# The last row tile of an expert's first group is summed and split six steps behind the second tile instead of eight

## The chip, the cores and the metric

The kernel runs on one core of a Trainium2 chip. The metric is the device time of one execution in microseconds (us); lower is better. The time before is 987.38 us, the median of three executions (985.54 to 989.09).

## The reference, cut to what matters

The kernel computes an attention layer with 32 memory slots per head, and then a mixture of eight experts over its 4608 output rows `x` of 512 numbers, of which each row uses two:

```python
for e in range(E):                       # E = 8
    for k in range(2):
        mask = top2[:, k] == e
        h = np.maximum(x[mask] @ w1[e], 0.0)          # 512 -> 1024
        out[mask] += top2_w[mask, k, None] * (h @ w2[e])   # 1024 -> 512
```

Only the expert part is touched by the change.

## The kernel before, in words

The rows of each expert are collected in a list of at most 1216 slots. In the experts 1 to 7 that list is worked off in two groups, written (e, g) here: group 0 has 640 rows, group 1 has 576. Each group goes through these stages.

**Gathering and splitting the rows** (`gather_sums`, line 908). A group is taken as two halves that are multiplied together, so it has 320 (group 0) or 288 (group 1) columns, in three row tiles: two of 128, and a last one of 64 (group 0) or 32 (group 1). For each row tile POOL gathers two blocks, `gsum` and `gtile` (L920). VectorE (DVE) forms sums for a seven-product scheme (L937, L938, L952, L953). Then the tile is split in three parts, each into a high and a low fp16 half: `ghalf` from `gsum` (the rows as they are), `ghalf` from `gtile` (after L938), and `gsplit` from `gsum` (after L952 and L953). ScalarE (ACT) makes the high half (L947), DVE the low half (L948), and the DMA queue of SP transposes both into the buffer `xt` (L949).

**First product** (`mm1_sums`, line 964). TensorE (PE) forms seven products for each of four column blocks, six matmuls for each, of 288 or 320 columns (L978). Product 1 and 2 read the part of `xt` that comes from `ghalf<-gsum`, products 7 and 4 read that from `ghalf<-gtile`, and products 6, 5 and 3 read that from `gsplit`. Product 1 opens a PSUM tile named `ps`, product 2 one named `pb`, product 7 one named `mp`; product 6 adds to product 1's `ps`. The tuple `ORDER` (line 83) starts with products 1, 1, 2, 6, 2, 6, 7, 7. ACT reads the sums out (`r`, `s`, `yv`: L984, L1026), DVE combines them (`yw`, `yv`: L988), and the result becomes a high half `hh` (ACT, L991) and a low half `hl` (DVE, L992).

**Second product** (`mm2`, line 1072). PE multiplies `hh` and `hl` by the second weights (L1092), ACT scales the row tile into `y` (L1104), and POOL adds it to the output rows (L1122).

**Weights.** The weights of the next expert are loaded by SP (L742, 512 KB each) and prepared by ACT (L782 takes squares, L792 the high half) and DVE (L785, L795 the low half); one small product on PE (L406) lies in that chain.

**What sets the order.** The main loop emits the first product of one group and the second product of the same group in steps; `step_side` counts them in `ticks[0]` and after each one lets one of the side generators (gathering for later groups, weight preparation) emit a piece. `gather_sums` holds a row tile back until `ticks[0]` has reached `moved`, which is set to the current tick plus `MOVE` (8) when the tile before it has been emitted. `pace` makes a piece's first instruction wait for a matmul that was emitted some three steps earlier. A scheduler then orders the instructions of each engine by priority and by its own estimate of time, so what stands in a row on an engine is not the order of emission; each engine then runs its row in that order.

```python
            n, a, b, t = fetched[i]
            yield from until(max(t, moved))
```

Of the kernel before, what the change touches and what calls it, by code (L numbers as in the profile page):

```python
# [80 lines left out]
LAG, STEP, WAIT, FAR, MOVE, MORE = 2, 100, 8, 8, 8, ()  # L81
# [10 lines left out]
def tile_attn_moe(ctx, tc, q_t, phi_t, kv, wgn, noise, w1, w2, out):  # L92
# [809 lines left out]
    def pace(d):  # L902
        if len(paced) > LAG:
            tc.add_manual_dep(d.ins, paced[-1 - LAG].ins.name, SYNC, reason="pace")
# [3 lines left out]
    def gather_sums(e, g, free):  # L908
        nh, t0 = HALF[g], 5 * g
        fetched = {}  # L910

        def fetch(i):
            if i > 2:
                return
            n = 128 if i < 2 else nh - 256
            a = late["gs"].tile([128, 768], F32, name="gsum", bufs=2)
            b = mpool.tile([128, DM], F32, name="gtile", bufs=GT)
            for x, ix in ((a[:, 256:768], LT[e][:n, t0 + i if i < 2 else t0 + 4, 0:1]),
                          (b, LT[e][:n, t0 + 2 + i, 0:1] if i < 2 else LX[e][:n, g, 0:1])):
                G.indirect_dma_start(out=x[:n], out_offset=None, in_=xs[:, :],  # L920
                                     in_offset=bass.IndirectOffsetOnAxis(ap=ix.bitcast(I32), axis=0))
            fetched[i] = (n, a, b, ticks[0] + FAR)

        fetch(0)
        yield
        while not free():
            yield "wait"
        xt = XT[e, g] = late["xt"].tile([128, NX, nh], F16, name="xt%d" % g)
        moved = 0
        for i in range(3):  # L930
            fetch(i + 1)
            yield
            n, a, b, t = fetched[i]
            yield from until(max(t, moved))
            s1, a11, a12 = (a[:n, k:k + 256] for k in (0, 256, 512))
            a21, a22 = b[:n, 0:256], b[:n, 256:512]
            pace(V.tensor_tensor(s1, a21, a22, OP.add))  # L937
            V.tensor_tensor(a21, a11, a21, OP.subtract)  # L938
            yield
            for x, k, w in ((a[:n, 256:768], 0, 2), (b[:n], 2, 2), (a[:n], 4, 3)):  # L940
                if k == 4:
                    gh = late["gs"].tile([128, 2, 768], F16, name="gsplit", bufs=2)[:n]
                else:
                    halves[0] += 1
                    gh = late["gs"] if halves[0] % 3 == 0 else mpool
                    gh = gh.tile([128, 2, DM], F16, name="ghalf", bufs=1 if halves[0] % 3 == 0 else 2)[:n]
                pace(A.activation(gh[:, 0], x, AF.Copy))  # L947
                V.tensor_tensor(gh[:, 1], x, gh[:, 0], OP.subtract)  # L948
                nc.sync.dma_start_transpose(xt[:, 4 * k:4 * k + 4 * w, i * 128:i * 128 + n], gh.rearrange("p a d -> p (a d)"))  # L949
                yield  # L950
                if k == 0:
                    V.tensor_tensor(a11, s1, a11, OP.subtract)  # L952
                    V.tensor_tensor(a12, a12, a11, OP.subtract)  # L953
                    yield
            moved = ticks[0] + MOVE

    banks = [0]

# [178 lines left out]
    side, paced, ticks = [], [], [0]  # L1137

    def until(t):
        while ticks[0] < t:  # L1140
            yield "wait"
# [160 lines left out]
    def rows_in(k, e, g):  # L1302
        return gather_sums(e, g, lambda: k < opened[0]) if e else gather(e, g)
# [96 lines left out]
```

## Time and profile before

| | |
|---|---|
| median of three executions | 987.38 us (985.54 to 989.09) |
| the profiled execution | 984.07 us, of which the span from first to last instruction is 982.1 us |
| busy share of the span | PE 93%, DVE 64%, ACT 59%, POOL 35% |
| granted TensorE clock, mean | 0.98 of full speed |

The attention part takes about the first 290 us; from there to about 955 us PE works through the fourteen groups of the experts 1 to 7 almost without a gap, and a short end follows in which POOL writes the last rows.

### The profile page before, as it was taken

The numbers are of one execution on the slowest core, as the hardware profiler recorded it, in microseconds if no ns is written. First come the engines' busy times: TensorE is split into PE (matmuls) and PEld (weight loads), VectorE is DVE, ScalarE is ACT, GpSimd is POOL, SyncE is SP. The second block draws the span as 40 slices with busy tenths as digits, with TensorE's granted clock in tenths as the row PEclk, the third lists the DMA queues.
The fourth block names the chain that finished last, engine by engine and source line by source line (L and its number), as shares of the span: only waits on it lengthen the run. The fifth ranks groups of instructions, "written<-read, shape, count | busy, mean of one in ns | idle before, by whom it ended". The sixth has DMA issues, their size and how long they took to land.

```text
span 982.1 us, 17769 instructions
## 1 busy us (share of the span) xinstructions
PE 917.5 (93%) x6510; PEld 544.4 (55%) x6510; DVE 626.4 (64%) x1471; ACT 579.8 (59%) x1188; POOL 342.5 (35%) x310
## 2 busy tenths in 40 slices
PE   3898985999899999999999999999999999999994
PEld 2465653677446564646564646464656465656552
DVE  1557788655677585849574957595759575957240
ACT  2586775433547575758665765576567665765240
POOL 3121654724243324535453232323242324240302
PEclk9999987999999999999999999999999999999998
DMA  8999989874878576947795689577947784775403
GB/s 317 323 333 313 362 272 328 239 101 101 153 180 162 110 147 128 212 75 158 132 201 101 140 122 201 91 149 132 208 72 170 137 180 77 169 110 82 63 1 49
DMA packets 197720, 162.03 MB, mean 165 GB/s; under 512 B 151872, under 2 KB 162304, under 8 KB 195584
## 3 DMA queue, kind: packets, MB, share of 16 engines
q1 hardware_dynamic: 177952, 120.43, 50.1%
q0 software_dynamic: 19680, 40.45, 23.5%
q8 instruction: 52, 0.85, 0.4%
q14 instruction: 36, 0.29, 0.1%
HBM read 86.77 MB, written 41.07 MB: 130 GB/s over the span
## 4 chain that ended last, share of the span: by engine, by line
PE 63%; DVE 5%; DMA 5%; issue 3%; ACT 2%; POOL 1%; SPq 0%; POOLq 0%; ACTq 0%
PE ps L1092 19%; PE mp L1092 15%; PE ps L978 14%; PE mp L978 7%; PE pb L978 4%; DMA xt<-ghalf 3%; PE mp L1062 3%; DVE wl L795 1%; DMA gtile<-xs,ltall 1%; DVE wlx L795 1%; POOL out L1122 1%; DVE yw L988 1%; DVE yv L988 1%; DVE gsplit L948 0%; ACT wl L782 0%
## 5 line engine op out<-in xcount | busy, mean ns | idle before, releaser
L1122 POOL DMA_INDIRECT out<-y,ltall x80 | 135.3, 1691 | 258.8 <-ACT y L1104 228.9
L1092 PEld LDWEIGHTS <-hh 128*128 128x128 f16 (+2 forms) x1504 | 122.7, 99 | 144.4 <-issue 17.5
L978 PE MATMUL ps<-xt,wh 128*128 128x320 f16 (+1 forms) x560 | 139.2, 293 | 1.1 <-ACT s L984 0.7
L1092 PE MATMUL ps<-wl,hh 128*128 128x512 f16 (+2 forms) x400 | 125.8, 380 | 0.0
L1092 PE MATMUL ps<-wh,hl 128*128 128x512 f16 (+2 forms) x400 | 125.5, 380 | 0.0
L1092 PE MATMUL ps<-wh,hh 128*128 128x512 f16 (+2 forms) x400 | 122.7, 381 | 0.0
L1092 PE MATMUL mp<-wh,hh 128*128 128x512 f16 (+2 forms) x352 | 113.4, 380 | 0.5 <-DVE hh L1069 0.5
L1092 PE MATMUL mp<-wl,hh 128*128 128x512 f16 (+2 forms) x352 | 113.0, 380 | 0.0
L1092 PE MATMUL mp<-wh,hl 128*128 128x512 f16 (+2 forms) x352 | 112.3, 380 | 0.0
L978 PEld LDWEIGHTS <-wh 128*128 128x128 f16 x896 | 86.6, 98 | 41.5 <-issue 5.8
L1092 PEld LDWEIGHTS <-hl 128*128 128x128 f16 (+2 forms) x752 | 63.2, 99 | 68.9 <-issue 4.9
L978 PE MATMUL ps<-xt,whx 128*128 128x320 f16 (+1 forms) x336 | 96.4, 292 | 0.0
L792 ACT ACTIVATE wh<-stg,wsc 128x512 f16<-128x512 f32 x112 | 76.4, 713 | 31.7 <-DVE wsc L415 20.0
L920 POOL DMA_INDIRECT gtile<-xs,ltall x28 | 34.5, 1233 | 138.8 <-DVE ghalf L948 133.5
L978 PEld LDWEIGHTS <-whx 128*128 128x128 f16 x672 | 65.7, 98 | 27.2 <-issue 2.7
L795 DVE SCALAR_TENSOR_TENSOR wl<-stg,wsc,wh 128x1024 f16<-128x1024 f32 (+1 forms) x63 | 73.1, 1160 | 10.6 <-ACT wh L792 10.2
L978 PE MATMUL ps<-xt,wl 128*128 128x320 f16 (+1 forms) x280 | 72.8, 292 | 0.0
L782 ACT ACTIVATE wl<-stg 128x1024 bf16<-128x1024 f32 x56 | 58.6, 1047 | 23.9 <-DMA stg<-in_w 18.7
L978 PE MATMUL mp<-xt,wh 128*128 128x320 f16 (+1 forms) x224 | 64.9, 293 | 4.1 <-DMA xt<-ghalf 4.1
L709 POOL DMA_INDIRECT lst<-gent,gidx x54 | 54.5, 1009 | 36.2 <-DVE gidx L692 18.5
L920 POOL DMA_INDIRECT gsum<-xs,ltall x42 | 46.3, 1103 | 55.4 <-DVE gsplit L948 44.8
L978 PE MATMUL mp<-xt,whx 128*128 128x320 f16 (+1 forms) x224 | 64.9, 292 | 0.0
(245 smaller groups left out, 1886.8 us busy)
## 6 DMA issues: line engine op xcount, KB each, us to landing
stg<-in_w SPq DMA_DIRECT2D x64, 512.0 KB
kvs<-in_kv SPq DMA_DIRECT2D x16, 1024.0 KB
out<-zt SPq DMA_DIRECT2D x38, 256.0 KB
qs<-in_q_t SPq DMA_DIRECT2D x16, 576.0 KB
xs<-xr SPq DMA_DIRECT2D x36, 256.0 KB
phs<-in_phi_t SPq DMA_DIRECT2D x16, 288.0 KB
kvs<-in_kv SPq DMA_DIRECT2D x16, 128.0 KB
xt<-ghalf SPq DMA_TRANSPOSE x88
```

The source lines that it names most:

```text
L709: sc = G.indirect_dma_start(out=lst[:, :], out_offset=bass.IndirectOffsetOnAxis(ap=idx[:, j, k:k + 1], axis=0), in_=ent[:, j, k, :], in_of ...
L782: (id if first else pace)(A.activation(wl[:, c * 1024:c * 1024 + 1024].bitcast(BF16), s[c], AF.Square, accum_out=am[:, c:c + 1]))
L792: (id if first else pace)(A.activation(h[:, o + k:o + k + 512], x[:, k:k + 512], AF.Identity, scale=sc))
L795: V.scalar_tensor_tensor(l[:, o:o + n], x, sc, h[:, o:o + n], op0=OP.mult, op1=OP.subtract)
L920: G.indirect_dma_start(out=x[:n], out_offset=None, in_=xs[:, :], in_offset=bass.IndirectOffsetOnAxis(ap=ix.bitcast(I32), axis=0))
L978: mark["pe"] = T.matmul(ps[:, :nh], t[w][:, o:o + 128], xt[:, 4 * k0 + 2 * n0 * lo + 2 * (a - k0) + c, :nh], start=(first and m == 0), sto ...
L988: V.scalar_tensor_tensor(y[:, h, :nh], ps[:, :nh], SHC, x[:, :nh], op0=OP.mult, op1=OP.add)
L1062: d = mark["pe"] = mark["mm1", g] = T.matmul(ps[:, :n], ww[:, c * FF + f * 128:c * FF + (f + 1) * 128], xt[:, xo + c, :n], start=(k == 0), ...
L1092: mark["pe"] = T.matmul(ps[lo:lo + x.shape[-1]], x, ws, start=start, stop=stop)
L1122: d = G.indirect_dma_start(out=out[:, :], out_offset=bass.IndirectOffsetOnAxis(ap=LT[e][:n, t, 0:1].bitcast(I32), axis=0), in_=y[:n], in_o ...
```

## The change

`moved` is the tick at which the next row tile may be summed and split. The changed line sets it when a tile has been emitted; `i` is that tile's number. With `i` equal to 1 the next one is the last tile of the group. The value for `i` equal to 2 is never used, since the next group starts with `moved = 0`. So one tile in each of six groups, (2,0) to (7,0), may be emitted two ticks earlier.

```diff
@@ gather_sums
-            moved = ticks[0] + MOVE
+            moved = ticks[0] + (6 if i and e > 1 and g == 0 else MOVE)
```

Since the scheduler sees other priorities and other matmuls to wait for, rows move on all engines from that point of the program on, also later tiles and weight preparation. Three places show it.

On ACT, ahead of group (3,0), stand the readouts of (2,1)'s first product (`yv`, `hh`), the squares of expert 3's second weights (L782), the scaled rows of (2,1) (L1104), and the splits (L947) of (3,0)'s last tile, which are those of 64 rows. Before:

```order
L1026 ACTIVATE yv<-ps_5781 128x288
L782 ACTIVATE wl_5939,wam<-stg_5930 128x1024
L991 ACTIVATE hh<-yw 128x2x288
L991 ACTIVATE hh<-yv 128x2x288
L991 ACTIVATE hh<-yw 128x2x288
L782 ACTIVATE wl_5939,wam<-stg_5934 128x1024
L1104 ACTIVATE y<-ps_5922,wlu 128x512
L782 ACTIVATE wl_5939,wam<-stg_5932 128x1024
L947 ACTIVATE gsplit<-gsum 64x768
L782 ACTIVATE wl_5939,wam<-stg_5936 128x1024
L1104 ACTIVATE y<-ps_6003,wlu 128x512
L947 ACTIVATE ghalf<-gtile 64x512
```

And in the changed kernel, at the same place:

```order
L991 ACTIVATE hh<-yv 128x2x288
L947 ACTIVATE ghalf<-gtile 64x512
L991 ACTIVATE hh<-yw 128x2x288
L1026 ACTIVATE yv<-ps_5783 128x288
L947 ACTIVATE ghalf<-gsum 64x512
L782 ACTIVATE wl_5943,wam<-stg_5934 128x1024
L991 ACTIVATE hh<-yv 128x2x288
L991 ACTIVATE hh<-yw 128x2x288
L782 ACTIVATE wl_5943,wam<-stg_5938 128x1024
L947 ACTIVATE gsplit<-gsum 64x768
L782 ACTIVATE wl_5943,wam<-stg_5940 128x1024
L1104 ACTIVATE y<-ps_5926,wlu 128x512
```

The split of `gtile` has moved from behind the second L1104 to the middle of the `hh` rows, that of `gsplit` from behind the first L1104 and the third L782 to behind the second L782. The `ghalf<-gsum` split of this tile stood seven rows above the first row shown of before, and now stands between the `hh` rows too.

On DVE, at the same place, stand the combined products and low halves of (2,1) (L988, L992) and the sums and low halves of (3,0)'s last tile (64 rows). Before:

```order
L992 SCALAR_TENSOR_TENSOR hl<-yv,hh 128x2x288
L988 SCALAR_TENSOR_TENSOR yw<-mp,s_5850 128x288
L992 SCALAR_TENSOR_TENSOR hl<-yw,hh 128x2x288
L992 SCALAR_TENSOR_TENSOR hl<-yv,hh 128x2x288
L992 SCALAR_TENSOR_TENSOR hl<-yw,hh 128x2x288
L937 TENSOR_TENSOR gsum<-gtile 64x256
L938 TENSOR_TENSOR gtile<-gsum,gtile 64x256
L952 TENSOR_TENSOR gsum<-gsum 64x256
L953 TENSOR_TENSOR gsum<-gsum 64x256
L948 TENSOR_TENSOR gsplit<-gsum,gsplit 64x768
L785 TENSOR_REDUCE wam_6067<-wam 128x1
L948 TENSOR_TENSOR ghalf<-gtile,ghalf 64x512
```

And in the changed kernel:

```order
L937 TENSOR_TENSOR gsum<-gtile 64x256
L938 TENSOR_TENSOR gtile<-gsum,gtile 64x256
L988 SCALAR_TENSOR_TENSOR yw<-mp,s_5832 128x288
L992 SCALAR_TENSOR_TENSOR hl<-yv,hh 128x2x288
L948 TENSOR_TENSOR ghalf<-gtile,ghalf 64x512
L988 SCALAR_TENSOR_TENSOR yw<-mp,s_5852 128x288
L992 SCALAR_TENSOR_TENSOR hl<-yw,hh 128x2x288
L948 TENSOR_TENSOR ghalf<-gsum,ghalf 64x512
L952 TENSOR_TENSOR gsum<-gsum 64x256
L953 TENSOR_TENSOR gsum<-gsum 64x256
L992 SCALAR_TENSOR_TENSOR hl<-yv,hh 128x2x288
L992 SCALAR_TENSOR_TENSOR hl<-yw,hh 128x2x288
```

Six of the last tile's rows now stand ahead of the last two `hl` rows; its `gsplit` follows directly behind the rows shown.

On ACT, ahead of group (2,0), the first group that the change touches, the changed kernel has these rows (the names are as above, one expert earlier):

```order
L991 ACTIVATE hh<-yv 128x2x288
L947 ACTIVATE ghalf<-gtile 64x512
L991 ACTIVATE hh<-yw 128x2x288
L782 ACTIVATE wl_4879,wam<-stg_4874 128x1024
L947 ACTIVATE ghalf<-gsum 64x512
L782 ACTIVATE wl_4879,wam<-stg_4876 128x1024
L1104 ACTIVATE y<-mp,wlu 128x512
L782 ACTIVATE wl_4879,wam<-stg_4872 128x1024
L1104 ACTIVATE y<-ps_4944,wlu 128x512
L947 ACTIVATE gsplit<-gsum 64x768
L1104 ACTIVATE y<-mp,wlu 128x512
```

Here `gsplit` has changed places with `ghalf<-gtile`: it stands behind the second L1104, where `ghalf<-gtile` stood before.

## Rows read from the trace of the kernel before

**Rows 1.** Page, part 1: busy time, share of the span, instructions.

```profile
PE 917.5 (93%) x6510; PEld 544.4 (55%) x6510; DVE 626.4 (64%) x1471; ACT 579.8 (59%) x1188; POOL 342.5 (35%) x310
```

**Rows 2.** Waits of PE, 290 to 955 us: total, times, longest.

```profile
PE mp L978 <- DMA xt<-ghalf: 4.1, 3, 1.8
PE ps L978 <- ACT s L984: 0.7, 3, 0.3
```

**Rows 3.** Timeline of PE: start, duration, instruction, idle before it.

```profile
397.28 0.30 PE L978 MATMUL mp<-xt,wh 128*128 128x320 f16 x1
...
489.33 0.45 PE L978 MATMUL ps<-xt,wh 128*128 128x320 f16 x2
...
492.68 0.31 PE L978 MATMUL mp<-xt,wh 128*128 128x320 f16 x1 [0.73 <-DMA xt<-ghalf]
...
590.75 0.31 PE L978 MATMUL mp<-xt,wh 128*128 128x320 f16 x1 [1.83 <-DMA xt<-ghalf]
...
782.25 0.31 PE L978 MATMUL mp<-xt,wh 128*128 128x320 f16 x1 [1.55 <-DMA xt<-ghalf]
```

**Rows 4.** Timeline of SP's queue ahead of (3,0): start and duration of issue.

```profile
471.62 0.53 SPq L742 DMA_DIRECT2D stg<-in_w  x1
483.79 1.23 SPq L949 DMA_TRANSPOSE xt<-gsplit  x1
485.66 1.30 SPq L949 DMA_TRANSPOSE xt<-ghalf  x1
```

**Rows 5.** Chain that ended last: start, duration, what.

```profile
485.66 6.97 DMA xt<-ghalf
...
582.20 8.50 DMA xt<-ghalf
...
774.75 7.46 DMA xt<-ghalf
```

**Rows 6.** Timeline of DVE ahead of (3,0).

```profile
470.93 0.45 DVE L988 SCALAR_TENSOR_TENSOR yw<-mp,s 128x288 f32<-128x288 f32 x1
...
474.85 0.75 DVE L992 SCALAR_TENSOR_TENSOR hl<-yw,hh 128x576 f16<-128x576 f32 x1
478.38 0.42 DVE L937 TENSOR_TENSOR gsum<-gtile 64x256 f32<-64x256 f32 x1 [2.78 <-PE ps L1092]
...
482.81 0.95 DVE L948 TENSOR_TENSOR gsplit<-gsum,gsplit 64x768 f16<-64x768 f32 x1 [2.66 <-ACT gsplit L947]
...
484.94 0.69 DVE L948 TENSOR_TENSOR ghalf<-gtile,ghalf 64x512 f16<-64x512 f32 x1 [0.94 <-ACT ghalf L947]
```

**Rows 7.** Timeline of ACT ahead of (3,0).

```profile
477.61 1.06 ACT L782 ACTIVATE wl<-stg 128x1024 bf16<-128x1024 f32 x1 [2.99 <-DMA stg<-in_w]
...
480.32 0.69 ACT L1104 ACTIVATE y<-ps,wlu 128x512 f32<-128x512 f32 x1 [1.57 <-PE ps L1092]
...
481.95 0.83 ACT L947 ACTIVATE gsplit<-gsum 64x768 f16<-64x768 f32 x1
...
484.29 0.62 ACT L947 ACTIVATE ghalf<-gtile 64x512 f16<-64x512 f32 x1
```

**Rows 8.** Timeline of ACT ahead of (4,0).

```profile
576.87 0.69 ACT L1104 ACTIVATE y<-ps,wlu 128x512 f32<-128x512 f32 x1 [1.63 <-PE ps L1092]
...
580.84 0.62 ACT L947 ACTIVATE ghalf<-gtile 64x512 f16<-64x512 f32 x1
```

**Rows 9.** Timeline ahead of and in (2,0): ACT, DVE, SP, PE.

```profile
389.37 0.62 ACT L947 ACTIVATE ghalf<-gtile 64x512 f16<-64x512 f32 x1
...
390.02 0.68 DVE L948 TENSOR_TENSOR ghalf<-gtile,ghalf 64x512 f16<-64x512 f32 x1 [0.94 <-ACT ghalf L947]
...
390.73 1.27 SPq L949 DMA_TRANSPOSE xt<-ghalf  x1
...
400.27 0.30 PE L978 MATMUL ps<-xt,wh 128*128 128x320 f16 x1
```

**Rows 10.** Chain that ended last, a gather of 128 rows.

```profile
201.10 4.50 DMA gtile<-xs,ltall
```

## The prediction

> **What bounds the kernel now.** I read the page first: PE is busy for 93% of the span, the next engine for 64% [rows 1]. A change on ACT, DVE or the DMA queues can then give time back only where PE waits, so the second view is PE's own waits. From 290 us to 955 us, in which all fourteen groups are worked off, there are two kinds: three waits for the transpose `xt<-ghalf`, 4.1 us together, and three of at most 0.3 us for a readout of ACT, 0.7 us together [rows 2]. That is the whole stock from which this change can pay: 4.8 us, of which 4.1 us are of the kind that it touches.
>
> The timeline of PE says where they lie [rows 3]. All three stand before the first matmul into `mp`, which is product 7, the first reader of what comes from `ghalf<-gtile`: 0.73 us in group (3,0), 1.83 us in (4,0), 1.55 us in (6,0). Product 1 and 2 ran ahead of it without a wait. The same matmul of (2,0) at 397.28 us shows no wait.
>
> **What the late transpose is late for.** I followed (3,0) backwards. The transpose that PE waits for is issued at 485.66 us [rows 4] and takes 6.97 us to land; the other two take 8.50 and 7.46 us [rows 5]. It is issued late because its split is: DVE makes the low half at 484.94 us, ACT the high half at 484.29 us [rows 6, 7]. ACT does so only then because its row has three L782, two L1104 and `gsplit` ahead of it (the order shown with the change). The first L1104 waits 1.57 us for PE's second product of the group before, and the second L782 2.99 us for its weights [rows 7]. DVE, meanwhile, stood idle for 2.78 us before L937 of this tile, until a matmul that `pace` had named [rows 6]. So of the last tile's three parts `ghalf<-gtile` comes last, although it is read before `gsplit`. (4,0) shows the same picture: `ghalf<-gtile` at 580.84 us, 3.97 us behind the start of the first L1104 at 576.87 us [rows 8].
>
> **What the change does there.** It adds and removes no work. The same seven DVE and three ACT instructions and three transposes of the tile stand elsewhere, and two things follow.
>
> *The order of need is restored.* In five of the six groups `gtile` is now split ahead of `gsplit`. In the sixth, (4,0), the two stand one behind the other, both ahead of the third L782 and of every L1104. In (3,0) and (6,0), too, all three splits stand ahead of the first L1104. The split that PE waited for was made at 484.29 us, the first L1104 began at 480.32 us [rows 7], so it comes at least 3.97 us earlier in (3,0), and the same 3.97 us in (4,0) [rows 8]; the waits to cover are 0.73 and 1.83 us [rows 3].
>
> *A closer reckoning for (3,0).* In DVE's new row L937 and L938 (0.42 us each) stand ahead of the `yw` that began at 470.93 us [rows 6]. With that `yw` (0.45) and one `hl` (0.75) the low half of `gtile` begins near 470.93 + 0.84 + 0.45 + 0.75 = 472.97 us and ends 0.69 us later, at 473.7 us, where before it ended at 485.6 us. Its transpose, even at 8.50 us, lands by 482.2 us, over 9 us before its reader. `gsplit` stands on ACT behind the second L782, which began at 477.61 us when its weights had landed: 477.61 + 1.06 + 0.2 (its accumulator read, about) + 0.83 on ACT, then 0.95 on DVE [rows 6, 7] is 480.7 us. At 8.50 us it lands at 489.2 us. In PE's new row product 6 of (3,0), the first reader of `gsplit`, stands behind 37 matmuls, product 7 behind 18. Without its wait product 7 began at 492.68 - 0.73 = 491.95 us [rows 3]; 19 matmuls at 0.136 us ((400.27 - 397.28) / 22, from (2,0) [rows 3, 9], where 22 lie between) put product 6 at 494.5 us. That leaves 5.3 us.
>
> *The tightest group is (2,0).* There `gsplit` takes the place behind the second L1104 that `ghalf<-gtile` had (389.37 us). It is longer by 0.83 - 0.62 on ACT and by 0.95 - 0.68 on DVE [rows 6, 7, 9], so it is issued near 390.73 + 0.21 + 0.27 = 391.2 us and lands, with 6.97 to 8.50 us, between 398.2 and 399.7 us. Its reader stands behind 42 matmuls, two more than before: 400.27 + 0.27 = 400.5 us [rows 9]. Cover: 0.8 to 2.3 us. I count no wait there.
>
> So the three waits go: -0.73 - 1.83 - 1.55 = -4.11 us.
>
> **What it may cost.** Six of the tile's DVE rows now stand ahead of the last two `hl` of the second product's input: 4 x 0.42 + 2 x 0.69 = 3.06 us; on ACT two `ghalf`, 2 x 0.62 us, stand among the `hh`. Whoever needs `hl` is PE's L1092. The cover is the idle time of DVE behind the last `hl` (474.85 us), 2.78 us [rows 6], and the fact that PE shows no wait for `hl` at all [rows 2]; how far it is from one no row shows. The bounds are nothing and, with no cover, 3.06 us in each of six groups, 18.4 us. I take the value from the nearest row: PE's existing short waits are of 0.3 us at most [rows 2], and I allow two such, 0.5 us, for rows that moved. SP and POOL issue the same transfers; the last tile's transposes now stand ahead of nothing that PE waits for, since the loads of the next weights follow them as before.
>
> Sum: the profiled execution took 984.07 us, span 982.1 us and 2.0 us around it. 984.07 - 4.11 + 0.5 = 980.5 us. The runs shown have a median of 987.38 us, 3.31 us above that execution; carried over, 987.38 - 3.6 = **983.8 us**, 0.36% less.
>
> **The rivals.**
>
> 1. *The landing doesn't follow the issue.* Two transposes of (3,0) are issued 1.87 us apart [rows 4], and all three late ones take 7 to 8.5 us [rows 5], whatever their place: other transfers are in flight. If the landing is set by these, an earlier issue only lengthens the flight, the waits stay, and the time is 987.4 us. For it speaks the spread of the flights; against it, that the earliest bound, the landing of the weights issued at 471.62 us, is past by 477.61 us, when L782 could begin [rows 4, 7], 14 us before the reader. The Trainium skill (DMA: Bandwidth & Descriptors, section Queues, rings and completion order) says that a transfer's semaphore step lands only after every earlier write of that DMA engine, across its queues. By that rule, the earlier transposes would still not be held past the weights' landing; that the flights are long while much is in flight agrees with it.
>
> 2. *The gain is given back further on.* The whole row of ACT behind (2,0) is reordered. In (5,0), (6,0) and (7,0) a first 128-row split of the following group now stands among the last tile's rows. ACT would be held by a gather that has just been issued. A gather took 4.50 us in the chain [rows 10]; less the 2.99 us by which ACT already stood idle at such a place [rows 7], that is 1.5 us each, 4.5 us in all: 984.07 - 3.6 + 4.5 = 985.0 us, that is 988.3 us on the runs' scale.
>
> 3. *The sums delay the second product* (slower). Place: the last two `hl` on DVE, ahead of L1092. Price: 3.06 us less the part that is covered, in six groups. It decides from 4.11 / 6 = 0.7 us uncovered per group on: at 1.3 us each (a cover of 1.8 us) it is 984.07 - 4.11 + 7.8 = 987.8 us, 991.1 us on the runs' scale. For it: DVE and ACT run in the order of their rows, and the second L782 of ACT held everything behind it for 2.99 us [rows 7]. Against it: the idle 2.78 us of DVE directly behind [rows 6], and no PE wait on DVE in the list [rows 2]. The Trainium skill (TensorE: Matmul & The Clock Gate, section Architectural detail: the array is 16x 32x32, not 1x 128x128) calls the queues of ScalarE and VectorE strictly first in, first out. By that rule whatever stands ahead of `hl` delays it; the trace agrees for ACT.
>
> **How the numbers follow.** I give the forecast 0.62, rival 1 0.12, rival 2 0.13, rival 3 0.13. About 0.3% (3 us) is what a measurement of this kernel can tell from no change. Of the forecast's 0.62 I leave 0.04 below that bound, since 3.6 us is close to it. Faster: 0.58. Same: 0.04 + 0.12 + 0.13 = 0.29. Slower: 0.13. The forecast's own range is 979.3 to 985.3 us: below, all 4.8 us of waits go and with them the 3.3 us that the runs lie above the profiled execution; above, half of the 4.11 us stays. With rivals 1 and 2, at 987.4 and 988.3 us, the range is 979.3 to 989.1 us, the slowest run of before; it leaves out rival 3 and a little of the forecast.
>
> **What would show it.** In the changed kernel's profile: PE's list of waits from 290 us on has no `xt<-ghalf` wait of over 0.3 us, and none for `gsplit` in (2,0). The last tile's `ghalf<-gtile` ends on DVE near 473 to 474 us before (3,0), and its transpose is no piece of the chain any more. (3,0) begins as early as before, (4,0) by 0.7 us and (5,0) by 2.6 us earlier. If the list shows waits for `hl` or `hh` in L1092, rival 3 holds; if for `s`, `r` or `yv` behind a split in (5,0) to (7,0), rival 2; if the transposes are issued early and still land at the old time, rival 1. What would make it wrong: a change of the row order of PE itself that costs it time that no wait of before hints at, or a part of the 3.31 us between the profiled execution and the runs that comes from these very waits, in which case the gain is larger.

## The result and the profile after

The changed kernel takes 975.5 us, the median of four executions (974.04 to 979.31), beside 986.46 us (984.37 to 989.09, four executions) of the kernel before in the same series: a ratio of 0.9893, with a 95% interval of 0.9854 to 0.9933. In a later series it was 976.43 us (11 executions) beside 983.55 us (22), a ratio of 0.9946 (0.9924 to 0.9969). So it is faster, by 0.5 to 1.1%. (The ratios with their intervals are estimates from the executions of a series, not quotients of the two medians beside them; in the later series the quotient would be 0.9928.) One slow execution of a kernel below, `c2_before_free`, is left out of its median and range: 984.54 us, 1.6% above its fastest. The forecast, 983.8 us, had the direction right and the size too small; 975.5 us lies below its range.

The page of the changed kernel, part 1, answers to [rows 1]:

```profile
PE 912.0 (93%) x6510; PEld 545.2 (56%) x6510; DVE 626.2 (64%) x1471; ACT 580.9 (59%) x1188; POOL 346.8 (35%) x310
```

The same 6510 matmuls keep PE busy for 5.5 us less. PE's waits from 290 to 955 us (total, times, longest) answer to [rows 2]:

```profile
PE mp L1092 <- DVE yw L988: 1.9, 1, 1.9
PE ps L978 <- ACT s L984: 1.6, 4, 0.7
PE ps L1092 <- DVE hl L992: 0.3, 1, 0.3
PE ps L1092 <- ACT hh L991: 0.2, 1, 0.2
```

All three waits for `xt<-ghalf` are gone, as forecast. But other waits have come, 4.0 us in all against 4.8 us before: by this list the change should have paid 0.8 us.

To see what it paid I cut out of each execution the stretch from the first matmul of (1,0) to that of (7,1), which leaves aside what comes before the change and the end. A row of this view has the stretch, its length, and then busy time and count of PE, PEld, DVE, ACT and POOL. Of the kernel before:

```profile
299.02:923.91 624.89, 619.71 (x4070) 360.19 (x4070) 423.74 (x776) 397.35 (x730) 215.67 (x157) 1.00 0.73 137
```

And of the changed kernel:

```profile
300.68:919.22 618.54, 614.36 (x4071) 361.31 (x4070) 423.03 (x776) 398.80 (x730) 220.25 (x157) 1.00 0.76 139
```

The stretch is 6.35 us shorter. Only 1.0 us of that is idle time of PE (624.89 - 619.71 = 5.18 us, now 4.18 us); 5.35 us are busy time, for the same matmuls at the same granted clock (1.00, third from the end of the row).

**Where busy time can shrink.** The second product of a group has a last row tile of 64 or 32 rows per half. Its 48 matmuls are narrow (64 or 32 columns of weights). From the start of (4,1) to that of (5,0) PE has no wait in either kernel, yet this took 683.80 - 637.63 = 46.17 us before and 680.19 - 635.26 = 44.93 us after. PE's timeline of the kernel before there (start, duration, instruction; neighbours alike are drawn together, xN; `128*32` means 32 columns of weights, `128*128` the full width):

```profile
637.10 0.38 PE L1092 MATMUL ps<-wh,hl 128*64 128x512 f16 x2
637.31 0.38 PE L1092 MATMUL ps<-wl,hh 128*64 128x512 f16 x2
637.63 0.42 PE L978 MATMUL ps<-xt,wh 128*128 128x288 f16 x2
...
666.51 0.40 PE L1092 MATMUL ps<-wh,hh 128*32 128x512 f16 x4
666.73 0.39 PE L1092 MATMUL ps<-wh,hl 128*32 128x512 f16 x4
666.95 0.38 PE L1092 MATMUL ps<-wl,hh 128*32 128x512 f16 x2
667.26 0.39 PE L1092 MATMUL mp<-wh,hh 128*128 128x512 f16 x1
...
671.47 0.39 PE L1092 MATMUL ps<-wh,hh 128*32 128x512 f16 x1
671.79 0.39 PE L1092 MATMUL mp<-wh,hl 128*128 128x512 f16 x1
...
683.80 0.45 PE L978 MATMUL ps<-xt,wh 128*128 128x320 f16 x2
```

And of the changed kernel, where all 48 stand together:

```profile
635.26 0.42 PE L978 MATMUL ps<-xt,wh 128*128 128x288 f16 x2
...
676.95 0.38 PE L1092 MATMUL mp<-wh,hl 128*128 128x512 f16 x1
677.17 0.38 PE L1092 MATMUL mp<-wl,hh 128*128 128x512 f16 x1
677.48 0.40 PE L1092 MATMUL ps<-wh,hh 128*32 128x512 f16 x4
...
679.86 0.39 PE L1092 MATMUL ps<-wl,hh 128*32 128x512 f16 x4
680.19 0.31 PE L978 MATMUL ps<-xt,wh 128*128 128x320 f16 x1
```

Two prices stand in these rows. Four narrow matmuls of 32 columns run side by side in one slot of 0.216 us ((679.86 - 677.48) / 11), the time of a single wide one, and so do two of 64 columns (637.10 to 637.31); a narrow one alone takes a whole slot too (671.47). And each change between wide and narrow takes 0.31 to 0.32 us from one start to the next instead of 0.216 us, so about 0.1 us more. Before, these 48 stood in five pieces; after, in one. In the order of PE's row the blocks of the twelve groups (1,0) to (6,1) stand in 39 pieces before and in 23 after (that of (7,0), the last one in the stretch, is one piece in both). None of this is a wait, so no list of waits shows it.

The Trainium skill (TensorEngine Tiling (Array Packing), section Key Properties) says that tiles of the array work in parallel and that a change of the tiling mode drains the engine. The rows above agree with both: four narrow matmuls share a slot of 0.216 us, and each change costs about 0.1 us.

### The profile page after: what moved, and what is told of

The parts are those of the page before. It is cut to its first block, busy times and chain, and to the rows that moved or that the text cites. A ratio compares the mean times of both kernels' runs of the same rounds, so it can differ in the third digit from the quotient of the medians.

```text
span 977.4 us, 17761 instructions
## 1 busy us (share of the span) xinstructions
PE 912.0 (93%) x6510; PEld 545.2 (56%) x6510; DVE 626.2 (64%) x1471; ACT 580.9 (59%) x1188; POOL 346.8 (35%) x310
## 4 chain that ended last, share of the span: by engine, by line
PE 69%; ACT 3%; issue 2%; DVE 2%; DMA 2%; POOL 1%; SPq 0%; POOLq 0%; ACTq 0%
PE ps L1092 20%; PE mp L1092 17%; PE ps L978 16%; PE mp L978 8%; PE pb L978 4%; PE mp L1062 3%; DMA xt<-ghalf 1%; ACT whx L792 1%; DMA gtile<-xs,ltall 1%; POOL out L1122 1%; ACT hh L991 1%; ACT ghalf L947 0%; DVE ghalf L898 0%; DVE wlx L795 0%; ACT yv L1026 0%
## 5 line engine op out<-in xcount | busy, mean ns | idle before, releaser
L1092 PEld LDWEIGHTS <-hh 128*128 128x128 f16 (+2 forms) x1504 | 122.9, 99 | 143.1 <-issue 14.1
L1122 POOL DMA_INDIRECT out<-y,ltall x80 | 133.3, 1666 | 185.0 <-ACT y L1104 154.9
L978 PE MATMUL ps<-xt,wh 128*128 128x320 f16 (+1 forms) x560 | 138.8, 293 | 1.6 <-ACT s L984 1.6
L1092 PE MATMUL ps<-wl,hh 128*128 128x512 f16 (+2 forms) x400 | 124.3, 379 | 0.0
L1092 PE MATMUL ps<-wh,hl 128*128 128x512 f16 (+2 forms) x400 | 123.5, 380 | 0.3 <-DVE hl L992 0.3
L1092 PE MATMUL ps<-wh,hh 128*128 128x512 f16 (+2 forms) x400 | 120.8, 381 | 0.2 <-ACT hh L991 0.2
L1092 PE MATMUL mp<-wh,hh 128*128 128x512 f16 (+2 forms) x352 | 111.9, 380 | 2.7 <-DVE yw L988 1.9
L1092 PE MATMUL mp<-wl,hh 128*128 128x512 f16 (+2 forms) x352 | 111.7, 379 | 0.0
L1092 PE MATMUL mp<-wh,hl 128*128 128x512 f16 (+2 forms) x352 | 111.1, 379 | 0.0
L978 PEld LDWEIGHTS <-wh 128*128 128x128 f16 x896 | 86.5, 98 | 37.3 <-issue 5.8
L1092 PEld LDWEIGHTS <-hl 128*128 128x128 f16 (+2 forms) x752 | 62.4, 99 | 68.2 <-issue 3.3
L978 PE MATMUL ps<-xt,whx 128*128 128x320 f16 (+1 forms) x336 | 96.9, 292 | 0.0
L920 POOL DMA_INDIRECT gsum<-xs,ltall x42 | 49.5, 1178 | 96.8 <-DVE gsplit L948 87.6
L978 PEld LDWEIGHTS <-whx 128*128 128x128 f16 x672 | 65.7, 98 | 27.9 <-issue 2.4
L920 POOL DMA_INDIRECT gtile<-xs,ltall x28 | 36.6, 1306 | 119.8 <-DVE ghalf L948 113.5
L978 PE MATMUL ps<-xt,wl 128*128 128x320 f16 (+1 forms) x280 | 72.8, 292 | 0.0
L782 ACT ACTIVATE wl<-stg 128x1024 bf16<-128x1024 f32 x56 | 58.7, 1049 | 22.5 <-PE ps L1092 10.9
L984 ACT ACTIVATE r<-ps 128x320 f32<-128x320 f32 (+1 forms) x112 | 46.0, 421 | 39.4 <-PE ps L978 30.2
L978 PE MATMUL mp<-xt,wh 128*128 128x320 f16 (+1 forms) x224 | 64.9, 292 | 0.0
```

The costliest lines, as they stand in the source:

```text
L782: (id if first else pace)(A.activation(wl[:, c * 1024:c * 1024 + 1024].bitcast(BF16), s[c], AF.Square, accum_out=am[:, c:c + 1]))
L978: mark["pe"] = T.matmul(ps[:, :nh], t[w][:, o:o + 128], xt[:, 4 * k0 + 2 * n0 * lo + 2 * (a - k0) + c, :nh], start=(first and m == 0), sto ...
L984: A.activation(y[:, :nh], ps[:, :nh], AF.Identity, scale=SHC)
L1092: mark["pe"] = T.matmul(ps[lo:lo + x.shape[-1]], x, ws, start=start, stop=stop)
L1122: d = G.indirect_dma_start(out=out[:, :], out_offset=bass.IndirectOffsetOnAxis(ap=LT[e][:n, t, 0:1].bitcast(I32), axis=0), in_=y[:n], in_o ...
```

## The experiments

The waits theory is that of the prediction: what the change pays is the waits for the late transpose. The rival is the row theory: most of it comes from PE's row, which happens to be cut less often. Eleven runs were made, nine of new kernels and one more of each of the two; none leaves out work.

**Rows tied: c1_before_tied and c1_after_tied.** A rule without a wait holds the 48 narrow matmuls of a group behind all that the group's other tiles emit, and the next 48 matmuls behind them. The first of its two functions is shown; the other one sets `tie` to the last narrow matmul and 48, and collects in `lasts` the last matmul of every other tile:

```diff
+    def row(d, last=None):
+        if last:
+            for x in [last] + lasts:
+                tc.add_manual_dep(d.ins, x.ins.name, ROW, reason="row")
+            lasts.clear()
+        elif tie[1]:
+            tc.add_manual_dep(d.ins, tie[0].ins.name, ROW, reason="row")
+            tie[1] -= 1
+        return d
```

Expected of the kernel before with this rule:

> The kernel before (MOVE 8), with the matmuls of each second product's last row tile (the narrow ones, of 32 or 64 columns of weights, L1092) kept in one piece on PE; the last gather tile is still split late. Row theory (most of the gain comes from PE's row: narrow matmuls that stand alone between wide ones cost a whole slot each): group-to-group intervals without a recorded wait fall from about 46.2 and 49.3 us to about 45.2 and 49.3 us, some 5 to 6.5 us in all, so about 980 us against 986.5 us of before, while waits for the transpose xt<-ghalf of up to 4 us remain. Wait theory (the gain is that of the three waits): the waits stay, so 986 us, within 0.3%.

Measured: 974.18 us (six executions), ratio 0.9915 (0.9884 to 0.9946) to the kernel before. With `MOVE` at 8 the tied row gives at least as much as the change. PE's busy time in the stretch is 614.23 us, as in the changed kernel. In one point both theories missed: no wait for `xt<-ghalf` is left, so the gain here is that of the row and of these waits together (PE's idle time in the stretch is 1.6 us, against 5.2 us). The tile is still emitted as late, but the last matmul that the split of `gtile` has to wait for now stands 86 matmuls ahead of the split's reader in PE's row instead of 74 to 80, since the rows around it moved too. The list of PE's waits there, the whole of it:

```profile
PE ps L978 <- ACT s L984: 1.6, 6, 0.3
```

Expected of the changed kernel with the rule:

> The changed kernel with the narrow matmuls of each second product's last row tile kept in one piece on PE. Row theory: the pieces that the changed kernel still has (in (1,1), (2,1), (3,1) and (6,1)) close, 2 to 4 us less than the changed kernel, 972 to 974 us. Wait theory: nothing that PE waits for changes, 975.5 us, within 0.3% of the changed kernel.

Measured: 975.23 us, ratio 0.9909 (0.9881 to 0.9937) to the kernel before. Busy time is 1.5 us lower (612.83 us, 18 pieces), but one wait of 2.0 us for `yv` fell into the profile; against the changed kernel itself the times don't tell them apart, so the 2 to 4 us that the row theory had put on it are not shown.

**Early tile, cut row: c1_move5.** Five steps instead of six happen to give 32 pieces.

```diff
-            moved = ticks[0] + MOVE
+            moved = ticks[0] + (5 if i and e > 1 and g == 0 else MOVE)
```

> The last tile five steps behind the second instead of six: its transposes are issued at least as early as in the changed kernel, but PE's row has the narrow matmuls in about as many pieces as before the change. Wait theory: no xt<-ghalf wait over 0.3 us, and the time of the changed kernel, about 975.5 us, or at least 4 us under before. Row theory: no xt<-ghalf wait either, but PE's busy time stays near the 917.5 us of before (changed kernel: 912.0 us), so 4 us of waits less and no more, 982 to 983 us; with new waits as in the changed kernel (3.3 us) 985 to 986 us.

Measured: 980.81 us, ratio 0.9971 (0.9948 to 0.9995), about half of the changed kernel's gain in the same series (0.9946). No wait for the transpose is left, so the waits theory wanted at least 4 us; the median is 2.7 us lower (its one profile has a stretch of 619.44 us, 4.9 us under the mean of the two of before). Busy time is not that of before, as the row theory had put it, but 2.9 us less in the stretch (617.00 us): with 32 pieces it stands between before and after.

**Second profiles: c1_after_again and c3_before_again.** The kernels unchanged.

> The changed kernel once more, for a second profile and more executions. If the profiled execution of 979.31 us was a slow draw of a program whose first 300 us vary, the experts' part from the first matmul of (1,0) to that of (7,1) is again 618.5 us within 0.5 us and the difference lies ahead of 300 us; the median is 974 to 977 us. If instead the expert part itself varies (waits that come and go), that stretch differs by 2 us or more.

> The kernel before, for a second profile. If its first profile is typical, the stretch from the first matmul of (1,0) to that of (7,1) is again 624.9 us within 1.5 us, with three waits for xt<-ghalf or a few more (in the other three groups the transpose landed 0.2 to 0.6 us ahead of its reader), and PE's busy time is 917.5 us within 1 us. If the median of before stands above its profiled execution because of these very waits, as the prediction had left open, they are 2 us or more longer here when the time is.

Measured, the changed kernel again, and then the kernel before again:

```profile
296.87:913.48 616.61, 614.29 (x4070) 361.07 (x4070) 422.86 (x776) 398.79 (x730) 220.08 (x157) 1.00 0.73 139
```

```profile
299.23:923.09 623.86, 620.07 (x4071) 359.82 (x4070) 423.62 (x776) 397.15 (x730) 215.62 (x157) 1.00 0.74 137
```

Busy time comes back within 0.4 us, so it belongs to the program and not to the draw; the waits don't come back so. The changed kernel's stretch is 1.9 us shorter than the first time, more than the 0.5 us expected. Its wait of 1.9 us for `yw` isn't there (idle time 2.3 us instead of 4.2), and the kernel before waits for `xt<-ghalf` in partly other groups, (4,0) to (7,0), and for other times:

```profile
PE mp L978 <- DMA xt<-ghalf: 2.6, 4, 0.7
```

The start of (1,0), ahead of which nothing differs, lies at 299.02 and 299.23 us in the kernel before and at 300.68 and 296.87 us in the changed one. That is where executions of one kernel differ by several us. By the means of two profiles each, the stretch is 624.4 us before and 617.6 us after: 6.8 us, or 0.69%, of which 5.6 us are busy time and 1.2 us waits. Both measured intervals hold 0.69%.

**The row whole, at 8, 6 and 15 steps: c2_before_free, c2_after_free, c2_late15_free.** Besides the rule above, L406 (the small matmul of the weight chain, which cut one block in nearly every group) is held ahead of the block:

```diff
-            T.transpose(pb[:, i, :], am[:, i:i + 1].to_broadcast([128, 128]), identf)
+            lasts.append(T.transpose(pb[:, i, :], am[:, i:i + 1].to_broadcast([128, 128]), identf))
```

In all three, every block is one piece. c2_late15_free also has 15 in place of the change's 6.

> The kernel before (MOVE 8) with the narrow matmuls of each second product's last row tile in one piece on PE, and with L406, the small matmul of the weight chain, ordered ahead of that piece instead of inside it. Row theory: the eleven pieces that L406 still cut close, at 0.38 us (64-column groups: 5.37 against 4.99 us for the piece) and 0.57 us (32-column groups: 2.96 against 2.39 us) each, some 5 us: the stretch from the first matmul of (1,0) to that of (7,1) goes from 615.8 us to about 611 us, and the time to about 970 us. Wait theory: no wait of PE is touched, so the stretch stays within 0.5 us of 615.8 us.

> The changed kernel (6 steps) with the same two rules on PE's row. PE's row is then in one piece in all groups, as in the kernel with MOVE 8 and the same rules, so the pair tells what the earlier tile is worth by itself. Row theory: nothing, since with the rows whole no transpose is late at MOVE 8 either: the two kernels within 1 us of each other. Wait theory: the earlier tile is 4 us better, since the waits for the transpose were what the change removed.

> The kernel before with whole rows on PE, and the last tile 15 steps behind the second instead of 8, so that its gtile split stands 74 rows of PE ahead of its reader, as in three groups of the kernel before. If the late transpose is a cost of its own, apart from PE's row, its waits return: up to 3 us in each of six groups, 5 to 18 us over the kernel with MOVE 8 and whole rows, while PE's busy time stays as low as there. If a whole row by itself is all that counts, the two are the same within 1 us.

| | time, us | ratio to before | stretch, us | PE busy in it |
|---|---|---|---|---|
| 8 steps, whole | 975.46 (969.27 to 979.12) | 0.9898 (0.9855 to 0.9941) | 622.18 | 611.98 |
| 6 steps, whole | 971.12 (968.21 to 974.18) | 0.9869 (0.9835 to 0.9903) | 612.24 | 610.18 |
| 15 steps, whole | 971.58 (971.23 to 972.04) | 0.9869 (0.9829 to 0.9908) | 612.84 | 609.98 |

Busy time did about what the row theory said, in all three. The time didn't: at 8 steps the stretch was 622 us, not 611 us, and against the row theory's "within 1 us of each other" the stretches at 8 and 6 steps differ by 10 us in the profiles, the medians by 4.3 us (the two intervals overlap, so the medians alone don't show it). The waits theory isn't right either, since hardly any of it is the transpose, and 15 steps, for which it had put 5 to 18 us more than for 8, are no slower than 6. PE's waits with 8 steps:

```profile
PE ps L978 <- ACT r L984: 9.0, 6, 3.2
PE mp L978 <- DMA xt<-ghalf: 1.0, 1, 1.0
```

And with 15 steps, where the tile is later still:

```profile
PE mp L978 <- DMA xt<-ghalf: 1.9, 3, 0.7
PE ps L1092 <- ACT hh L991: 0.7, 2, 0.5
PE mp L1092 <- ACT hh L991: 0.2, 1, 0.2
```

The timeline of the first, at the longest of the waits for `r`, in (2,0):

```profile
387.39 0.97 POOL L920 DMA_INDIRECT gsum<-xs,ltall  x1 [11.22 <-DVE gsplit L948]
...
389.11 1.95 POOL L1122 DMA_INDIRECT out<-y,ltall  x1 [0.75 <-ACT ghalf L947]
...
394.87 0.69 ACT L1104 ACTIVATE y<-ps,wlu 128x512 f32<-128x512 f32 x1 [5.45 <-DMA out<-y,ltall]
...
398.64 0.44 ACT L984 ACTIVATE r<-ps 128x320 f32<-128x320 f32 x1
399.13 0.30 PE L978 MATMUL ps<-xt,wh 128*128 128x320 f16 x1 [3.23 <-ACT r L984]
399.27 0.30 PE L978 MATMUL ps<-xt,whx 128*128 128x320 f16 x1
...
399.68 0.47 PE L978 MATMUL ps<-xt,wh 128*128 128x320 f16 x1
399.95 0.47 PE L978 MATMUL ps<-xt,whx 128*128 128x320 f16 x1
```

Read backwards: PE waits for ACT's `r`; ACT stood 5.45 us at L1104, because its `y` buffer was still being written out; that write stood on POOL behind a gather, and the gather 11.22 us for the last tile's `gsplit` to free its buffer. So the late tile reaches PE by a second way, over POOL and ACT. And the wait costs more than itself: right behind it, PE's granted clock is 0.50 from 400 to 403 us (the lower of its two levels, 1.2 instead of 2.4 GHz), and matmuls of 320 columns begin 0.27 us apart (399.68, 399.95) instead of 0.14 us (399.13, 399.27). For thirteen of them that is about 1.7 us, nearly all of the 1.8 us by which PE's busy time at 8 steps exceeds that at 6.

**That way tested: c3_before_free_f8 and c3_after_free_f8.** The gather of the next group's second tile is emitted eight steps later, so that writes stand ahead of it on POOL:

```diff
         for i in range(3):
+            yield from until(0 if i or e < 2 else ticks[0] + 8)
             fetch(i + 1)
```

> MOVE 8 with whole rows on PE, as in the second call, but the gather of the next group's second tile (L920, POOL) is put into the program eight steps later, so that POOL has the writes of the second product (L1122) ahead of it. Theory of the queue: with whole rows at MOVE 8, PE waited 9.0 us for r because ACT was held at L1104 for its y buffer (28.7 us, six times), that because the write of y stood on POOL behind a gather that waited up to 11.22 us for the last tile's gsplit to free its buffer. Then the waits for r fall from 9.0 us to under 2 us, ACT's waits for the write from 28.7 us to under 10 us, the stretch from (1,0) to (7,1) from 622.2 us to 612 to 615 us, and the time to 970 to 973 us. Wait theory (the late tile's split itself holds up ACT): nothing on POOL matters, the waits for r stay and the time is that of the kernel without the edit.

Measured: 983.37 us, ratio 0.9978 (0.9953 to 1.0003). PE's waits for `r` did fall from 9.0 to 1.3 us and ACT's for the write from 28.7 to 10.6 us, so the way over POOL is shown for most of these waits. But the time isn't better: the tiles gathered later are now late themselves, at product 1, and the stretch is 621.44 us.

```profile
PE ps L978 <- DMA xt<-ghalf: 6.7, 3, 2.7
PE ps L978 <- ACT r L984: 1.3, 2, 0.7
```

> The same edit on the changed kernel with whole rows, where POOL's gather is not held so long. Theory of the queue: little to win, within 1 us of the stretch of 612.2 us and of 971.1 us; a loss of 1 to 3 us if the gather that comes later makes the next group's rows late. Wait theory: the same as without the edit.

Measured: 977.63 us, ratio 0.9906 (0.9865 to 0.9947), a stretch of 620.84 us with two waits for transposes of 2.7 and 3.0 us in (2,0). The loss was larger than either expectation: 8.6 us of the stretch, of which 2.9 us are busy time. Behind the wait of 2.7 us the granted clock is 0.50 once more (396.2 to 399.4 us), behind that of 3.0 us it stays at 1.00.

**The price of a cut by itself: c2_broken.** The kernel with 6 steps and whole rows, but in the experts 3 and 4 two narrow matmuls alternate with one wide one of the tile before; the diff shows how tile 3's matmuls are drawn in:

```diff
                 for hs, ws in terms(f):
                     products(0, hs, ws, k == 0, k == 8 * m - 1)
                     k += 1
+                    if fine and k < 24:
+                        yield
+                    if other:
+                        next(other)
```

> The same as the changed kernel with whole rows, but in the experts 3 and 4 the narrow matmuls of the last row tile stand in twos between single wide matmuls of the tile before it, in all four groups; the work is the same. Row theory, with two prices: each change between wide and narrow costs 0.1 us (0.31 against 0.216 us from one start to the next), and in the 32-column groups, where four narrow matmuls share a slot of 0.216 us when they stand together, twos need twice the slots. So the interval of (3,0) and of (4,0) grows by some 46 x 0.1 = 4.6 us, that of (3,1) and (4,1) by 4.6 + 12 x 0.216 = 7.2 us, 23.6 us in all. Wait theory: the same 6510 matmuls with no new wait of PE, so no difference over 1 us.

Measured: 999.4 us (two executions), ratio 1.0152 (1.0101 to 1.0203). PE's timeline there:

```profile
582.01 0.39 PE L1092 MATMUL mp<-wh,hl 128*32 128x512 f16 x2
582.34 0.39 PE L1092 MATMUL ps<-wh,hh 128*128 128x512 f16 x1
582.66 0.39 PE L1092 MATMUL mp<-wl,hh 128*32 128x512 f16 x2
```

0.32 us from start to start, every time. The intervals of (3,0) and (4,0) grow by 5.2 us (54.29 against 49.06 us; expected 4.6), those of (3,1) and (4,1) by 8.6 and 8.9 us, of which 1.1 us each is a new wait of L406, so 7.5 and 7.8 us (expected 7.2). Busy time in the stretch rises from 610.18 to 635.98 us. For the same work and the same 6 steps, the order of PE's row makes 25.8 us of busy time.

All kernels, sorted by the pieces of the twelve blocks:

| kernel | pieces | PE busy in the stretch, us | PE idle in it, us |
|---|---|---|---|
| c2_broken | 104 | 635.98 | 5.6 |
| before (two profiles) | 39 | 619.71, 620.07 | 5.2, 3.8 |
| c1_move5 | 32 | 617.00 | 2.4 |
| c1_before_tied | 24 | 614.23 | 1.6 |
| changed (two profiles) | 23 | 614.36, 614.29 | 4.2, 2.3 |
| c1_after_tied | 18 | 612.83 | 4.3 |
| c3_before_free_f8 | 14 | 611.52 | 9.9 |
| 8, 6, 15 steps, whole | 12 | 611.98, 610.18, 609.98 | 10.2, 2.1, 2.9 |
| c3_after_free_f8 | 12 | 613.09 | 7.8 |

Busy time follows the pieces, at (619.9 - 610.2) / 27 = 0.36 us for each (0.28 us for the short ones of c2_broken); the 16 pieces that the change saves come to 5.8 us, and 5.6 us were measured. The two highest of the five values at 12 pieces are those with a stretch at the lower clock. Idle time follows no such order.

## Why the prediction was wrong

**The step that failed** is in its first part: that the change "can then give time back only where PE waits", made into a sum, "That is the whole stock from which this change can pay: 4.8 us." A PE that is busy for 93% was taken as a PE whose busy time is fixed, so the change's effect on PE's own row was costed at nothing. The row was worth 5.6 us of the 6.8 us. The prediction had named "a change of the row order of PE itself" among the things that would make it wrong, but only as a loss ("that costs it time"), and gave it neither a price nor a chance. It could have: the order of PE's row in the two programs shows 39 and 23 pieces, and the timeline of before has the price in plain sight, 0.31 us at a change and 2 or 1 in a slot for 4.

**The late transpose: right in its mechanism.** The waits for it are gone in both profiles of the changed kernel. Rival 1 fell: the transposes are issued earlier, and no reader waits for them. Ahead of (3,0) DVE's low half of `gtile` ends at 472.6 us (473.7 forecast, 485.6 before, [rows 6]), and the transposes go out from 472.61 us instead of 485.66 us [rows 4]:

```profile
471.90 0.68 DVE L948 TENSOR_TENSOR ghalf<-gtile,ghalf 64x512 f16<-64x512 f32 x1
```

```profile
472.61 2.83 SPq L949 DMA_TRANSPOSE xt<-ghalf  x2
```

(2,0), called the tightest, has no wait for `gsplit`. Counted from the start of (1,0), (4,0) begins 1.8 us and (5,0) 5.3 us earlier than before, where 0.7 and 2.6 us had been forecast: the rest is not the transpose's. But 4.11 us, read from one execution, was itself a draw: a second one had 2.6 us.

**New waits: too small.** 0.5 us was allowed; of other waits than that for the transpose there were 4.0 us in the profile (2.1 us in the second) where before had 0.7 us, so 3.3 and 1.4 us more. The largest is rival 2, at one of the three places that it named, ahead of (7,0):

```profile
842.33 1.25 POOL L920 DMA_INDIRECT gsum<-xs,ltall  x1 [4.51 <-DVE gsplit L948]
850.36 0.63 ACT L947 ACTIVATE ghalf<-gsum 128x512 f16<-128x512 f32 x1 [4.64 <-PE ps L978]
...
853.79 0.81 DVE L988 SCALAR_TENSOR_TENSOR yw<-mp,s 128x288 f32<-128x288 f32 x2
854.29 0.40 PE L1092 MATMUL mp<-wh,hh 128*32 128x512 f16 x4 [1.86 <-DVE yw L988]
```

ACT's split of the next group's first tile stands ahead of the readouts and begins 8.0 us after the gather was issued (the rival had put 4.50 us on a gather). The row names PE's L978, but in the second profile, with the same order, the split begins 5.9 us after the gather and PE doesn't wait; that it is the gather's landing is read from this, and no run took it away. Rival 3 came to 0.5 us (waits for `hl` and `hh` in L1092).

**Net of waits, then**, the sum's -4.11 + 0.5 became -1.2 us by two profiles each.

**The scale was off too.** The sum was carried up by 3.31 us to a median of three executions, 987.38 us. Later medians of the kernel before were 983.55, 984.29 and 985.59 us (22, 11 and 17 executions), so most of that step was the luck of three draws, and it moved forecast and range the wrong way. (The bound of 985.3 us also leaves out the 0.5 us of its own sum; nothing hangs on it.)

**What the earlier tile is worth alone** has no single answer: with rows tied, 8 and 6 steps are alike (974.18 and 975.23 us); with L406 held ahead as well, 6 steps are better by some 4 us in the medians, with intervals that overlap, and 15 steps as good as 6. At 8 steps it was which rows of POOL and ACT stood behind the tile's that decided; that this is so in general is read from these few kernels, each of which reshuffles those rows.

The fastest kernels here are the changed one with whole rows, 971.12 us, 0.9869 (0.9835 to 0.9903) of the kernel before, and that with 15 steps, which the times don't tell apart from it, where the changed kernel itself had 0.9893 and 0.9946 in its two series.

## What to carry to other kernels

When an engine is the bound, its busy time isn't a constant: compare the order of its own instructions before and after, and look in its timeline for places where small instructions share a slot, before any list of waits is summed up as all there is to win. An edit meant for one engine goes through a scheduler that may reorder all of them, so a gain can be due to a neighbour of the edit; tie down the order that isn't meant to change and measure again. And take two profiles: what repeats (here busy time, within 0.4 us) can be costed, while a wait of 1 or 2 us seen once may be a draw.

## What the runs showed of the hardware

- Four matmuls with 32 columns of weights, or two with 64, take one slot of 0.216 us when they stand together, as long as one with 128; two with 32 or a single one between wide ones take a whole slot too. A change between narrow and wide costs 0.1 us.
- A queue of POOL that was held by one gather (11.22 us) reached PE as a wait of 3.23 us, which ended 11.7 us after the gather began, by way of a write behind it and ACT's buffer.
- Behind that wait, and behind one of 2.7 us in `c3_after_free_f8`, PE's granted clock stood at 0.50 (1.2 GHz) for 3 us or more, with matmuls of 320 columns 0.27 us apart instead of 0.14 us; behind waits of 3.0 us there and 1.83 us in the kernel before [rows 3] it stayed at 1.00.
